# Talking-heads attention with a PReLU block behind it: four shared two-bank PSUM tiles in place of four dedicated ones, full-tile units in the second phase, contiguous group columns, 12 setup loads

## Chip, cores and metric

One core of one Trainium2 chip. The metric is the device time of one execution in microseconds (us). Engines: PE (TensorE: matmuls, its weight loads listed as PEld), DVE (VectorE), ACT (ScalarE), POOL (GpSimd), SP (SyncE, here only a DMA queue).

## What is computed

```python
batch, n_heads, seq, head_dim = (4, 12, 448, 64)
scores = scale * np.matmul(q, k.transpose(0, 1, 3, 2))
scores = np.einsum('bhij,hg->bgij', scores, w_pre)
scores = scores - np.max(scores, axis=-1, keepdims=True)
attn = np.exp(scores)
attn = attn / (np.sum(attn, axis=-1, keepdims=True) + 1e-09)
attn = np.einsum('bhij,hg->bgij', attn, w_post)
x = np.matmul(attn, v)            # then (1792 tokens) x (12 * 64 = 768)
h = x @ w_in                      # 768 x 2048
g = np.maximum(h, 0.0) + alpha * np.minimum(h, 0.0)
out = g @ w_out                   # 2048 x 768
```

The two weights `w_in` and `w_out` come as 64-bit floats, which the kernel rounds to fp32 itself; `q`, `k`, `v`, `w_pre`, `w_post` are fp32.

## The kernel before

The work has two phases that are interleaved by hand: every engine runs its instructions in the order in which the program lists them.

**First phase (attention)**: 90 steps `step(n)`; a step handles one batch of two groups of 10 query rows with all 12 heads. A step has on PE `mix(n)` (L188: the `w_pre` product, from `sr` tiles that DMAs of the SP queue, `relay`, have rearranged), `post(n-1)` (L222: the `w_post` product of the step before, which also divides by the sum), and, when due, `qk` (L160: scores of a chunk of 60 rows, three calls per chunk, placed by the table `qk_at`) and `pv` (L241: the product with `v`, two halves, some steps after a list of chunks is complete). Each is read out of PSUM by another engine: `rmax` (DVE, L193, one per step) and `exp` (ACT, L200) read `mix`; `post_out` (ACT, L231, two copies with strided columns) reads `post`; `qk_out` (L167) and `pv_out` (L249 and L250) read `qk` and `pv`. `norm(n)` (DVE, L206 to L210) makes the factors `r` that `post(n)` multiplies by, and needs the sums of `exp(n)`.

**Second phase (the two-layer block)**: the tokens are cut into four blocks `TB` (300, 498, 498, 496). A block can start when the attention rows it needs are stored to DRAM (`READY`); while the steps run, `moe_work` gives it a share of PE per step, `PACE`, in ns at full clock. Block 0 (`moe0`) multiplies in fp32, the others (`moe`) in three fp32r products with weights split into two parts (`split_w`: ACT cast L306, POOL subtract L307). The first layer (`l1`, L342 or L381) accumulates one of 16 column slices `f` and is read by DVE and ACT (L312, L394 to L396: the PReLU and the split of `g`); the second (`l2`, L360 or L408) accumulates for two slices one of 6 output slices `c` at a time, and DVE adds the result to `acc` (`add_out`, L320). One such piece is called a unit here. While the steps of `n <= ready[0]` run (the lead), no second-phase work is done, and `converts` rounds weights on DVE and POOL (L58 to L65). The last block can only run after the last step.

**PSUM** is eight banks in four tiles of two banks, each with its own use:

```python
PM = ps.tile([128, 2, 512], F32, name="m")     # mix
PS_ = ps.tile([128, 2, 512], F32, name="s")    # qk, first half of pv
PA = ps.tile([128, 2, 512], F32, name="pa")    # post, second half of pv
PW = ps.tile([128, 2, 512], F32, name="h")     # second phase (odd mixes in the lead)
banks = [PW[:, 0], PW[:, 1]]                   # a unit takes one bank, in turn
```

After the last step the other tiles' banks join the list, so that block 3 goes through eight banks in turn.

Of the kernel before, what the change touches and what calls it, by code (L numbers as in the profile page):

```python
# [22 lines left out]
HI = 5  # L23
HP = HI * H
# [12 lines left out]
WARM = (12, 8)  # L37
# [5 lines left out]
PACE = (3800.0, 5000.0, 5200.0)  # L43
CONV_LEAD, CONV_T0 = 4, 8
F0 = 8

# [22 lines left out]
def talking_heads_prelu(ctx: ExitStack, tc: tile.TileContext, q, k, v, w_pre, w_post, mask, w_in, w_out, alpha, out):  # L69
# [8 lines left out]
    groups = [(ci, g) for ci, (b, c) in enumerate(chunks) for g in range(CHUNKS[c][1] // GI)]  # L78
# [5 lines left out]
    for b, lists in enumerate(PVS):  # L84
        for cs in lists:
            r0 = CHUNKS[cs[0]][0]
            cn = sum(CHUNKS[cs[-1]]) - r0
            base = AW - cn if lists[-1] == cs == (len(CHUNKS) - 1,) else 0
            for c in cs:
                a_col[place[b, c]] = base + CHUNKS[c][0] - r0  # L90
            pvs.append((b, r0, cn, base, lb[place[b, cs[-1]]]))
# [92 lines left out]
    def mix(n, to):  # L184
# [40 lines left out]
    def post_out(n):  # L225
        for g in range(2):
            ci, j = groups[2 * n + g]
            nh = CHUNKS[chunks[ci][1]][1] // HI
            cols = a_t.rearrange("p s h i -> p (s h) i")[:, :, a_col[ci]:a_col[ci] + nh * HI]
            dst = cols.rearrange("p s (i u) -> p s u i", u=nh)[:, :, 2 * j:2 * j + 2]  # L230
            nc.scalar.copy(dst, PA[:, g, :NS * GP].rearrange("p (s u i) -> p s u i", u=2, i=HI))  # L231

    def pv(i, hx, to):
        b, r0, cn, base, _ = pvs[i]
        for cl in range(3):
            for s in range(NS):
                for t in range(2):
                    h = 2 * (3 * hx + cl) + t
                    for r in range(2 if 2 * s + 1 < NJ else 1):
                        pr = slice(64 * r, 64 * r + 64)  # L240
                        nc.tensor.matmul(to[64 * t:64 * t + 64, r, cl * AW:cl * AW + cn],  # L241
                                         v_t[b, hx][pr, s, (2 * cl + t) * D:(2 * cl + t + 1) * D],
                                         a_t[pr, s, h, base:base + cn], start=(s == 0), stop=(2 * s + 2 + r >= NJ))

    def pv_out(i, hx, to):
        b, r0, cn, base, _ = pvs[i]
        xe = xep.tile([128, 3, AW], F32, tag="xe", name=f"xe{i}_{hx}")
        src = to[:, :, :3 * AW].rearrange("p r (c i) -> p r c i", c=3)
# [39 lines left out]
    turn = [0]  # L288
# [389 lines left out]
```

## Time and profile before

| | us |
|---|---|
| median of 3 runs | 1534.86 (1532.36 to 1535.69) |
| profiled execution | 1545.28 |
| its span | 1543.5 |
| mean granted TensorE clock | 0.802 of 2.4 GHz |
| busy: PE, DVE, ACT, POOL | 1106.9, 560.2, 472.4, 397.0 |

The profiled execution is 0.7% above the median of the runs, and 1.8 us above its own span. PE is the busiest engine; its busy time is at the clock granted, which has two levels, 1.2 and 2.4 GHz, so that the same matmul can stand there with one duration or with twice that.

### The profile page before, as it was taken

What the parts mean: (1) busy time and instruction counts of PE and PEld (TensorE: products, weight loads), DVE (VectorE), ACT (ScalarE), POOL (GpSimd) and SP (SyncE); (2) the same over time, 40 slices, a digit from 0 to 9 for tenths busy, and PEclk for the clock granted to TensorE, in tenths of its full rate; (3) what the DMA queues carried; (4) which work ended last, traced back from release to release, by engine and by line L of the source; (5) the groups of instructions that cost most, each with busy time, mean ns of one, the idle gap of its engine ahead of it and who ended that gap; (6) DMA issues with size and microseconds to landing.
All of it is one profiled execution on the core that took longest, in us unless ns stands there. A gap on an engine that the chain in (4) does not pass through costs nothing. (4 is left out here: it accounts for less than half of the span.)

```text
span 1543.5 us, 28060 instructions
## 1 busy us (share of the span) xinstructions
PE 1106.9 (72%) x12012; PEld 727.5 (47%) x12012; DVE 560.2 (36%) x969; ACT 472.4 (31%) x837; POOL 397.0 (26%) x433
## 2 busy tenths in 40 slices
PE   3566555786776676877778777787877867687777
PEld 1244323453433434545445545554554645465555
DVE  2767645223434323222223333323232233233333
ACT  1344413232221223443323432343333322131111
POOL 6423433011111101222202322312221212243431
PEclk6668778788866877878768897697876879789999
DMA  6655665232323223422212322422221201322211
GB/s 156 225 177 191 193 220 161 99 111 71 108 90 111 83 95 113 121 69 90 73 35 84 111 69 91 149 75 78 69 75 43 90 28 52 113 68 78 72 51 40
DMA packets 73899, 155.45 MB, mean 101 GB/s; under 512 B 25700, under 2 KB 55408, under 8 KB 73776
## 3 DMA queue, kind: packets, MB, share of 16 engines
q0 software_dynamic: 20032, 84.29, 19.5%
q1 hardware_dynamic: 52812, 67.96, 12.6%
q8 instruction: 94, 1.54, 0.4%
q10 hardware_dynamic: 932, 1.43, 0.3%
q14 instruction: 29, 0.24, 0.0%
HBM read 91.33 MB, written 23.59 MB: 74 GB/s over the span
## 5 line engine op out<-in xcount | busy, mean ns | idle before, releaser
L307 POOL TENSOR_TENSOR ws<-wr,ws 128x768 fp32r<-128x768 f32 x96 | 175.7, 1831 | 657.8 <-ACT ws L306 656.9
L231 ACT COPY at<-pa 128x480 f32<-128x480 f32 x180 | 168.4, 1041 | 524.8 <-PE pa L222 524.8
L408 PE MATMUL h<-g,ws 128*128 128x498 f32 (+1 forms) x666 | 224.0, 482 | 90.7 <-DVE acc L320 52.0
L381 PE MATMUL h<-xs,ws 128*128 128x498 f32 (+1 forms) x612 | 205.9, 493 | 67.0 <-DVE t L394 33.2
L408 PEld LDWEIGHTS h<-g,ws 128*128 128x128 f32 x666 | 144.7, 231 | 167.5 <-DVE acc L320 79.1
L381 PEld LDWEIGHTS h<-xs,ws 128*128 128x128 f32 x612 | 141.9, 243 | 131.8 <-issue 34.9
L160 PE MATMUL s<-k,q 64*64 64x448 f32 x752 | 115.9, 656 | 82.6 <-ACT st L167 67.0
L320 DVE TENSOR_TENSOR acc<-h,acc 128x498 f32<-128x498 f32 (+2 forms) x139 | 85.3, 614 | 245.3 <-PE h L408 174.3
L222 PEld LDWEIGHTS pa<-r,e 64*64 64x64 f32 x5040 | 115.8, 155 | 110.7 <-issue 82.9
L222 PE MATMUL pa<-r,e 64*64 64x60 f32 x5040 | 117.9, 243 | 51.5 <-DVE r L210 42.0
L193 DVE TENSOR_REDUCE nm<-m 128x2 f32<-128x896 f32 x82 | 89.3, 1090 | 172.4 <-PE m L188 172.4
L188 PE MATMUL m<-sr,wk 64*64 64x448 f32 (+1 forms) x656 | 104.9, 698 | 0.0
L200 ACT ACTIVATE e<-m,nm 128x448 f32<-128x448 f32 x164 | 102.2, 636 | 6.8 <-DVE nm L193 6.8
L167 ACT COPY st<-s 128x896 f32<-128x896 f32 x87 | 80.2, 922 | 65.3 <-DMA sr<-st 33.5
L306 ACT CAST ws<-wr 128x768 fp32r<-128x768 f32 x96 | 78.0, 840 | 68.6 <-issue 56.9
L300 POOL DMA_DIRECT2D wr<-wsc x112 | 62.6, 560 | 110.6 <-PE h L360 51.3
L395 ACT CAST g<-t 128x498 fp32r<-128x498 f32 (+1 forms) x48 | 29.2, 609 | 172.5 <-DVE t L394 172.5
L160 PEld LDWEIGHTS s<-k,q 64*64 64x64 f32 x752 | 27.1, 153 | 104.3 <-ACT st L167 83.9
L206 DVE TENSOR_SCALAR s<-se 128x2 f32<-128x2 f32 x90 | 19.3, 215 | 148.7 <-ACT e L200 148.5
L360 PE MATMUL h<-g,w 128*128 128x300 f32 x96 | 45.9, 620 | 31.6 <-DVE acc L320 20.8
L59 POOL TENSOR_SCALAR ce<-ce 128x768 int32<-128x768 int32 x32 | 32.0, 999 | 139.3 <-DVE ce L58 136.9
L381 PE MATMUL m<-xs,ws 128*128 128x496 f32 x252 | 59.6, 389 | 9.8 <-DVE t L394 9.8
(86 smaller groups left out, 1204.0 us busy)
## 6 DMA issues: line engine op xcount, KB each, us to landing
wr<-wsc POOLq DMA_DIRECT2D x112, 384.0 KB, 3.6
sr<-st SPq DMA_DIRECT2D x330, 105.0 KB
cr<-in_w_in_dram POOLq DMA_DIRECT2D x16, 768.0 KB, 5.3
cr<-in_w_out_dram POOLq DMA_DIRECT2D x16, 768.0 KB, 5.3
wsc<-w SPq DMA_DIRECT2D x32, 384.0 KB
q<-in_q_dram POOLq DMA_DIRECT2D x54, 90.0 KB, 3.8
v<-in_v_dram POOLq DMA_DIRECT2D x8, 576.0 KB, 6.3
x<-xe SPq DMA_DIRECT2D x24, 180.0 KB
```

The lines of the kernel that those rows point to most:

```text
L160: nc.tensor.matmul(pt[64 * cc:64 * cc + 64, r, :S], q_t[ci][h, (3 * cc + p) * cn + SR0 * cc:(3 * cc + p) * cn + SR0 * cc + 64], k_t[b, p][ ...
L167: copy(s_t[ci][:, :, p, :], pt[:, :, :S])
L188: nc.tensor.matmul(to[hf:hf + 64, u, :S], wk[r, :], g[r, :], start=True, stop=True)
L193: nc.vector.tensor_reduce(out=nm, in_=m_t[n][:, :, :S], axis=AX.X, op=ALU.max, negate=True)
L200: nc.scalar.activation(out=e_t[n][:, u], in_=m_t[n][:, u, :S], func=AF.Exp, bias=nm_t[n][:, u:u + 1], scale=1.0, accum_out=se_t[n][:, u:u ...
L222: nc.tensor.matmul(dst[:, :, HI * u:HI * u + HI], e[h, u, 64 * jb:64 * jb + 64], r[h, u].rearrange("p (h i) -> p h i", h=H), start=True, s ...
L231: nc.scalar.copy(dst, PA[:, g, :NS * GP].rearrange("p (s u i) -> p s u i", u=2, i=HI))
L306: nc.scalar.copy(t[:, 0], w)
L307: nc.gpsimd.tensor_tensor(t[:, 1], w, t[:, 0], ALU.subtract)
L320: nc.vector.tensor_tensor(acc_o[:, c, :N], pt[:, :N], acc_o[:, c, :N], ALU.add)
L381: nc.tensor.matmul(pt[:, :N], w[:, tw, c * 128:(c + 1) * 128], xs[:, tx, c, :], start=(j == 0), stop=(j == 3 * NCC - 1))
L408: nc.tensor.matmul(pt[:, :N], w[:, tw, c * 128:(c + 1) * 128], g[:, tg], start=(j == 0), stop=(j == 3 * FG - 1))
```

## The change

Four two-bank tiles `p0` to `p3` replace the dedicated ones. `grab()` gives the one that was freed longest ago in program order, `free()` gives it back right after its readers are listed. A unit of the second phase fills a whole tile: `l1` takes two slices `f`, `l2` two output slices `c`, with one DVE instruction over both banks to add them; `order()` puts `l2` of a pair one pair of `l1` later. The columns of a group lie next to each other in `at`, so that `post` is read out by one ACT copy for both groups where they belong to one chunk (88 of the 90 steps; the un-permuting moves to the read-out of `pv`). In a step `exp(n)` now always follows `post(n-1)`, `norm(n)` stands behind two thirds of the step's second-phase work, and `qk` is not placed in steps with `pv`. The setup loads go from 28 to 12, two memsets go to POOL, the first `qk` stands ahead of `wk`, and fewer of the first relays go through ACT's queue. Pace, conversion rate and ready steps change too.

```diff
-PACE = (3800.0, 5000.0, 5200.0)
-CONV_LEAD, CONV_T0 = 4, 8
+PACE = (4200.0, 5600.0, 5600.0)
+CONV_LEAD, CONV_T0 = 4, 4
...
+    pairs = [ps.tile([128, 2, 512], F32, name=f"p{i}") for i in range(4)]
+    age = [0, 1, 2, 3]
+    clock = [4]
+    def grab():
+        i = min((i for i in range(4) if age[i] is not None), key=lambda i: age[i])
+        age[i] = None
+        return pairs[i]
+    def free(t):
+        age[next(i for i in range(4) if pairs[i] is t)] = clock[0]
+        clock[0] += 1
...
+    def mix(n):
+        to = m_t[n] = grab()
...
+        nc.vector.tensor_reduce(out=nm, in_=to[:, :, :S], axis=AX.X, op=ALU.max, negate=True)
...
+        free(m_t.pop(n))            # in exp(n)
...
+        if ca == cb:                # in post(n)
+            col = a_col[ca] + GI * ja
+            nc.scalar.copy(at[:, :, col:col + 2 * GI].rearrange("p q (g i) -> p g q i", g=2),
+                           pt[:, :, :NS * GP].rearrange("p g (q i) -> p g q i", i=GI))
...
     def add_out(t, G, c, pt, N):
+        dst = acc_o[:, c:c + 2, :N]
         if G == 0:
-            nc.scalar.copy(acc_o[:, c, :N], pt[:, :N])
+            nc.vector.tensor_copy(dst, pt[:, :, :N])
         else:
-            nc.vector.tensor_tensor(acc_o[:, c, :N], pt[:, :N], acc_o[:, c, :N], ALU.add)
+            nc.vector.tensor_tensor(dst, pt[:, :, :N], dst, ALU.add)
+        free(pt)
...
+        seq = [("l1", 0), ("l1", 1)]
+        for G in range(NG2 - 2):
+            seq += [("l2", G), ("l1", G + 2)]
+        return seq + [("l2", NG2 - 2), ("l2", NG2 - 1)]
...
+                pt = grab()         # moe, l1
+                for f in fs:
...
+                            nc.tensor.matmul(pt[:, f % 2, :N], w[:, tw, c * 128:(c + 1) * 128], xs[:, tx, c, :],
...
+                        for f1 in fs:
+                            prelu(P, t, f1, pt, N)
+                        free(pt)
...
+                for c in range(0, NCC, 2):          # moe, l2
+                    pt = grab()
+                    for d in range(2):
...
+                                nc.tensor.matmul(pt[:, d, :N], w[:, tw, (c + d) * 128:(c + d + 1) * 128], g[:, tg],
...
-    ready = [pvs[i][4] + 2 for i in READY]
+    ready = [pvs[i][4] + 3 for i in READY]
...
-                for i in range(HI):
-                    nc.gpsimd.dma_start(out=wb[o + NP * i:o + NP * i + NP, 0, :], in_=pre[c])
+                nc.gpsimd.dma_start(out=wb[o:o + HP // 2, 0, :], in_=wide(w_pre[NP * c:NP * c + NP], NP))
...
+            if live(n):             # in step(n)
+                mix(n)
             if due is not None:
...
             if live(n - 1):
                 post(n - 1)
...
+            if live(n):
                 exp(n)
...
+            else:
+                moe_work(n, pace * 0.4)
+                if cur == 0:
+                    converts(min(CONV_T0 // 2, room()))
+                moe_work(n, pace * 0.25)
             if live(n):
                 norm(n)
...
-                moe_work(n, pace)
+                moe_work(n, pace * 0.35)
```

How this moves instructions, at three places. First PE, in the second layer of block 1. Names: `m`, `pa`, `s`, `h` are the dedicated tiles, `p_119` to `p_122` the shared ones. Before:

```order
L188 MATMUL m<-sr_113,wk 64x448 x2
L222 MATMUL pa<-r_4697,e_4636 64x12x5 x28
L160 MATMUL s<-k_2_3843,q_114 64x448 x4
L408 MATMUL h<-g_0_4413,ws_1_4488 128x498 x3
L408 MATMUL h<-g_1_4509,ws_1_4499 128x498 x3
...
L381 MATMUL h<-xs_4367,ws_0_4516 128x498 x6
L188 MATMUL m<-sr_106,wk 64x448 x2
```

Now:

```order
L172 MATMUL p_122<-k_2_3779,q_114 64x448 x4
L410 MATMUL p_121<-xs_4345,ws_0_4551 128x498 x18
L442 MATMUL p_119<-g_0_4558,ws_1_4574 128x498 x3
L442 MATMUL p_119<-g_1_4564,ws_1_4590 128x498 x3
...
L200 MATMUL p_120<-sr_106,wk 64x448 x2
L200 MATMUL p_120<-sr_107,wk 64x448 x2
L233 MATMUL p_122<-r_4696,e_4647 64x12x5 x28
L172 MATMUL p_121<-k_0_3530,q_115 64x448 x4
```

Before, every row of the second phase writes `h`, three units of six matmuls there in a row. Now neighbouring pieces on PE write different tiles, and a unit of the second layer has twelve matmuls.

Second DVE, in a step of block 1 with second-layer units. Before:

```order
L206 TENSOR_SCALAR s_5336<-se_5273 128x2
L207 RECIPROCAL s_5336<-s_5336 128x2
L210 TENSOR_TENSOR r_5339<-wq,s_5336 128x120
L320 TENSOR_TENSOR acc<-h,acc 128x498 x2
L193 TENSOR_REDUCE nm_5365<-m 128x2
```

Now:

```order
L202 TENSOR_REDUCE nm_5281<-p_122 128x2
L342 TENSOR_TENSOR acc<-p_119,acc 128x2x498
L342 TENSOR_TENSOR acc<-p_121,acc 128x2x498
L216 TENSOR_SCALAR s_5349<-se_5313 128x2
L217 RECIPROCAL s_5349<-s_5349 128x2
L220 TENSOR_TENSOR r_5352<-wq,s_5349 128x120
L202 TENSOR_REDUCE nm_5362<-p_122 128x2
```

The adds now stand ahead of the three instructions of `norm`, which wait for ACT's sums, instead of behind them.

Third POOL, the setup. Before (these rows come twice):

```order
L462 DMA mask_sb<-in_mask_dram 30x1x60
L464 DMA wb<-in_w_pre_dram 6x1x12 x5
L462 DMA mask_sb<-in_mask_dram 30x1x60
L464 DMA wb<-in_w_pre_dram 6x1x12 x5
L466 DMA mask_sb<-in_mask_dram 60x60
L467 DMA wb<-in_w_post_dram 60x1x12
```

Now (the two `30`-row loads come four times, the other two twice):

```order
L502 MEMSET mask_sb 128x120
L503 MEMSET wb 128x24
L509 DMA mask_sb<-in_mask_dram 30x1x60
L510 DMA wb<-in_w_pre_dram 30x1x12
...
L513 DMA mask_sb<-in_mask_dram 60x60
L514 DMA wb<-in_w_post_dram 60x1x12
```

Five loads of 6 rows have become one of 30.

## Rows read from the trace of the kernel before

**Rows 1.** Busy time of each engine by stretch, whole core, cut at row maxima (L193); last columns: granted clock, DMA share, GB/s.
```profile
0.00:48.30 48.30, 18.73 (x84) 7.05 (x84) 17.43 (x35) 4.91 (x5) 29.82 (x52) 0.68 0.59 159
48.30:188.20 139.90, 79.78 (x1664) 52.40 (x1664) 95.05 (x149) 61.73 (x118) 48.50 (x62) 0.75 0.62 196
188.20:592.80 404.60, 279.01 (x3344) 165.90 (x3344) 152.17 (x275) 110.16 (x207) 70.76 (x95) 0.78 0.37 116
592.80:969.60 376.80, 289.73 (x3188) 190.39 (x3192) 116.76 (x208) 136.23 (x238) 94.25 (x94) 0.82 0.28 85
969.60:1308.80 339.20, 262.28 (x2851) 179.55 (x2845) 102.16 (x186) 114.81 (x203) 75.21 (x68) 0.79 0.24 74
1308.80:1355.00 46.20, 31.70 (x349) 21.93 (x339) 14.64 (x27) 8.84 (x15) 9.50 (x8) 0.76 0.35 105
1355.00:1543.50 188.50, 145.71 (x563) 110.26 (x562) 62.04 (x92) 35.67 (x52) 68.94 (x55) 0.93 0.21 61
```

**Rows 2.** The same view for L193 alone: length, DVE busy (xcount = steps), clock, DMA.
```profile
48.30:188.20 139.90, 18.41 (x17) 0.75 0.62 196
188.20:592.80 404.60, 29.43 (x27) 0.78 0.37 116
592.80:969.60 376.80, 26.17 (x24) 0.82 0.28 85
969.60:1308.80 339.20, 22.89 (x21) 0.79 0.24 74
```

**Rows 3.** PE's groups by line, 593 to 970 us: xcount | busy, mean ns | idle before, releasers.
```profile
L408 PE MATMUL h<-g,ws 128*128 128x498 f32 x288 | 100.5, 496 | 44.6 <-DVE acc L320 23.8 <-DVE t L394 15.6 <-ACT acc L318 3.6
L381 PE MATMUL h<-xs,ws 128*128 128x498 f32 x288 | 89.6, 462 | 24.6 <-DVE t L394 9.6 <-ACT ws L306 4.9 <-DVE acc L320 4.6
```

**Rows 4.** Timeline of one step in block 2: start us, us, engine line op, [idle before <-releaser].
```profile
1250.21 1.88 ACT L231 COPY at<-pa 128x480 f32<-128x480 f32 x2 [2.97 <-PE pa L222]
...
1253.25 0.17 DVE L206 TENSOR_SCALAR s<-se 128x2 f32<-128x2 f32 x1 [2.76 <-ACT e L200]
...
1253.86 0.67 DVE L320 TENSOR_TENSOR acc<-h,acc 128x498 f32<-128x498 f32 x1
...
1254.58 2.86 PE L408 MATMUL h<-g,ws 128*128 128x498 f32 x6 [2.86 <-DVE acc L320]
...
1258.21 2.86 PE L408 MATMUL h<-g,ws 128*128 128x498 f32 x6 [0.77 <-DVE acc L320]
```

**Rows 5.** Timeline in block 3, after the last step, where units go through eight banks.
```profile
1418.19 1.63 PE L408 MATMUL s<-g,ws 128*128 128x496 f32 x6 [2.13 <-DVE acc L320]
...
1419.66 1.50 PE L408 MATMUL pa<-g,ws 128*128 128x496 f32 x6
...
1419.86 0.68 DVE L320 TENSOR_TENSOR acc<-s,acc 128x496 f32<-128x496 f32 x1 [1.72 <-PE s L408]
```

**Rows 6.** One round of block 3 (two slices f), whole core, columns as in the first group.
```profile
1404.57:1427.10 22.53, 17.23 (x73) 13.22 (x72) 8.13 (x12) 4.25 (x7) 9.56 (x8) 1.00 0.25 71
```

**Rows 7.** Timeline of the start.
```profile
12.71 2.78 POOL L464 DMA_DIRECT2D wb<-in_w_pre_dram  x5
...
20.24 0.22 DVE L473 SCALAR_TENSOR_TENSOR wk<-mask_sb,wb 128x60 f32<-128x60 f32 x1 [13.48 <-DMA wb<-in_w_pre_dram]
...
35.80 0.91 ACT L167 COPY st<-s 128x896 f32<-128x896 f32 x1 [24.11 <-DMA sr<-st]
```

**Rows 8.** PE's groups by line, 48 to 188 us (the lead).
```profile
L222 PE MATMUL pa<-r,e 64*64 64x60 f32 x896 | 24.7, 268 | 44.4 <-DVE r L210 36.4 <-ACT st L167 4.9 <-DVE xe L250 3.0
```

**Rows 9.** ACT's groups by line and shape, whole span: two copies out of PSUM.
```profile
L231 ACT COPY at<-pa 128x480 f32<-128x480 f32 x180 | 168.4, 1041 | 524.8 <-PE pa L222 524.8
...
L167 ACT COPY st<-s 128x896 f32<-128x896 f32 x87 | 80.2, 922 | 65.3 <-DMA sr<-st 33.5 <-PE s L160 31.8
```

**Rows 10.** Timeline in block 3: the first and the last DVE step of one slice's PReLU.
```profile
1408.83 0.73 DVE L312 TENSOR_SCALAR t<-m,alpha_sb 128x496 f32<-128x496 f32 x1 [3.38 <-PE m L381]
...
1410.94 0.68 DVE L396 TENSOR_TENSOR g<-t,g 128x496 fp32r<-128x496 f32 x1 [0.67 <-ACT g L395]
```

More of the change, by code (lines that the diff above doesn't have):

```diff
@@ L77, in talking_heads_prelu @@
     place = {bc: ci for ci, bc in enumerate(chunks)}
-    groups = [(ci, g) for ci, (b, c) in enumerate(chunks) for g in range(CHUNKS[c][1] // GI)]
+    half = lambda ci: CHUNKS[chunks[ci][1]][1] // HI
+    groups = [(ci, g) for ci in range(len(chunks)) for g in range(half(ci) // 2)]
     NG, NC = len(groups), len(chunks)
@@ L287, in talking_heads_prelu @@
     wr_t, wi_t, wo_t, g_t, xs_t, xr_t = {}, {}, {}, {}, {}, {}
-    turn = [0]
-    banks = [PW[:, 0], PW[:, 1]]
-    def bank():
-        turn[0] += 1
-        return banks[turn[0] % len(banks)]
+    used, nxt_x = [0, 0], {}
     def load_w(u, x):
@@ L303, in split_w @@
     def split_w(P, u, x):
+        if (u, x) not in wr_t:
+            return
         t = P[x].tile([128, 2, DM], F32R, tag="w", name=f"ws{u}_{x}")
@@ L308, in split_w, with prelu @@
         (wi_t, wo_t)[x][u] = t
[L310 removed]
+    def prelu(P, t, f, pt, N):
         h = tp.tile([128, 512], F32, tag="t", name=f"t{t}_{f}")
[L312 to L313 removed]
+        ps_f = pt[:, f % 2, :N]
+        nc.vector.tensor_scalar(out=h[:, :N], in0=ps_f, scalar1=0.0, scalar2=alpha_sb[:, f:f + 1], op0=ALU.min, op1=ALU.mult)
+        if t == 0:
+            g = P["g"].tile([128, N], F32, tag="g", name=f"g0_{f}")
+            nc.vector.scalar_tensor_tensor(out=g, in0=ps_f, scalar=0.0, in1=h[:, :N], op0=ALU.max, op1=ALU.add)
+        else:
+            g = P["g"].tile([128, 2, N], F32R, tag="g", name=f"g{t}_{f}")
+            nc.vector.scalar_tensor_tensor(out=h[:, :N], in0=ps_f, scalar=0.0, in1=h[:, :N], op0=ALU.max, op1=ALU.add)
+            nc.scalar.copy(g[:, 0], h[:, :N])
+            nc.vector.tensor_tensor(g[:, 1], h[:, :N], g[:, 0], ALU.subtract)
+        g_t[t, f] = g
@@ L421, in split_x @@
         a, N = TB[t]
+        while step_now[0] <= ready[t]:
+            yield
         xs = xs_t[t] = P["xs"].tile([128, 2, NCC, N], F32R, tag="xs", name=f"xs{t}")
@@ L452, in talking_heads_prelu @@
         nc.vector.memset(warm.bitcast(F32), 0.0)
-        for _ in range(WARM[0]):
-            nc.tensor.matmul(PM[:, 0, :], warm[:, :128], warm, start=True, stop=True)
-        nc.vector.memset(mask_sb, 0.0)
-        nc.vector.memset(wb, 0.0)
-        pre = w_pre.rearrange("(r c p) g -> c r p g", r=2, c=2)
+        for _ in range(WARM):
+            nc.tensor.matmul(pairs[3][:, 0, :], warm[:, :128], warm, start=True, stop=True)
+        nc.gpsimd.memset(mask_sb, 0.0)
+        nc.gpsimd.memset(wb, 0.0)
         own = mask[:HP, :HI, :].rearrange("(i h) j g -> i h j g", h=H)
+        wide = lambda w, n: w.rearrange("(o h) g -> o h g", o=1).to_broadcast([HI, n, H])
         for u in range(2):
@@ L482, in talking_heads_prelu @@
         )
-        for p in range(3):
-            pt = qk(0, p, (PS_, PA, PM)[p])
-            qk_out(0, p, pt, nc.vector.tensor_copy if p % 2 else nc.scalar.copy)
-        load_q(2)
+        load_q(1)
         nc.gpsimd.dma_start(out=alpha_sb, in_=alpha)
@@ L492, in relays @@
             nonlocal relayed
-            while relayed < min(upto, NG):
+            while relayed < min(upto, NG) and (groups[relayed][0], NP // 2 - 1) in done_qk:
                 relay(relayed, dmas)
                 relayed += 1
-        relays(2 * (RA + 1) if lb[0] >= RA else 2 * lb[0] + 2, (nc.sync, nc.scalar))
+        relays(4, (nc.sync, nc.scalar))
+        relays(2 * (RA + 1), (nc.sync,))
         next(conv)
-        for hx in range(2):
-            load_v(0, hx)
+        for ci in (2, 3):
+            load_q(ci)
         conv_done, conv_steps, lead_steps = 0, NFC * 2 * 5, F0 * 2 * 5
@@ L558, in step @@
         def step(n):
-            for ci, p in qk_at.get(n, []):
-                if p == 0 and ci + 2 < NC:
-                    load_q(ci + 2)
+            step_now[0] = n
+            if n == 1:
+                for hx in range(2):
+                    load_v(0, hx)
             if n >= 0:
```

304 lines of the change are left out of this document (145 added, 159 removed).

## The prediction

> **What bounds the kernel now.** I read the busy time by stretch first, cut where the stages change [rows 1]: the start to the first row maximum, the lead (17 steps), the steps with block 0 (27), block 1 (24) and block 2 (21), a short change-over, and block 3 alone; the same view for L193 counts the steps [rows 2]. The reader is to see that PE is the busiest engine from 188 us on, but only for 69 to 77% of each stretch, and mostly at a mean granted clock of 0.78 to 0.82. Busy time times clock is what PE would need at 2.4 GHz without a pause: block 0 279.0 x 0.78 = 218 us of 404.6, block 1 289.7 x 0.82 = 238 of 376.8, block 2 262.3 x 0.79 = 207 of 339.2, block 3 145.7 x 0.93 = 136 of 188.5. No other engine is over 40% there. So the loss is pauses and a slow clock on PE, and what makes them is the question.
>
> The groups by line say who ends the pauses [rows 3]: in the block 1 stretch PE idles 44.6 us before L408 and 24.6 before L381, of 87 in all (376.8 - 289.7), mostly for DVE's reads, `acc` and `t`. The timeline shows it happening. Every second-layer unit on `h` waits 0.77 us for DVE's add of the unit before [rows 4], although the two lie in different banks: the wait is for the tile. Block 3 proves that: the second unit on `s` waits for the add, the next one, on `pa`, starts at 1419.66 while the add of `s` only starts at 1419.86 [rows 5]. Once per step it is worse: the add stands on DVE behind `norm`, `norm` waits for ACT's `exp`, `exp` stands behind the two copies of `post`, and PE pauses 2.86 us [rows 4]. After that pause six matmuls take 2.86 us, where they take 1.63 in block 3: PE is back at 1.2 GHz, and with 0.77 us lost after each unit it is still there two units later.
>
> The lead is another matter: DVE is busy 95.1 of 139.9 us there, PE 79.8, and PE's largest wait is for `r` of `norm` [rows 1, 8]. And the start is a chain of small loads: `wk` waits 13.48 us for `wb`, whose loads POOL issues at about 0.56 us each, and ACT's next copy waits 24.11 us behind relays [rows 7].
>
> **The change part by part.** All against the profiled execution (1545.3 us, span 1543.5; the median of the runs is 0.7% lower).
>
> *Setup.* 16 loads fewer on POOL at 2.78 / 5 = 0.56 us are 9 us [rows 7]; the first score copies no longer stand behind `wk`, and two of six groups leave ACT's relay queue. I take the start from 48.3 to 26 us; bounds 22 (all of the 24.11 us wait, and 2 more) and 40 (the 9 us alone).
>
> *The lead* is one step longer (ready + 3 for + 2), so 18 steps to the first with block 0. A step is 139.9 / 17 = 8.2 us now. Conversions stay on DVE; the two 1.04 us copies of `post` become one of 960 elements. The contiguous runs have no row; the bounds are 960 / 896 x 0.92 = 0.99 us, as the contiguous copy of scores goes, and 2 x 1.04 = 2.08 [rows 9]. I take 1.3, nearer to the first, since what differs from it (runs of ten) is small; 0.8 us less between `post` and `exp`, of which I credit 0.6: 18 x 7.6 = 137 us (117 to 148).
>
> *Blocks 0 to 2.* A tile is taken again only after three others, so PE has another piece between a unit and its tile's reuse: the 0.77 us waits go, and so do the equal ones between two first-layer slices. The read of a pair costs at most two adds of 0.68 us, 1.36 [rows 5], less than the 12 matmuls of the next pair. The adds now stand ahead of `norm`, and `norm` has a third of the step's second-phase work behind it, so the 2.86 us pause should go too. What is late next: the PReLU of a pair is twice a chain of DVE, ACT and DVE, 2.8 us for one slice [rows 10], and `rmax` and the `post` copy queue behind it. When the tile ring comes round to that tile first, PE waits some 1.4 us, and `post` may wait another 1 us for a late `norm`. That happens in about one step of three; with smaller waits elsewhere I put 1 us of pause on each step (bounds 0.3, and half of the present idle). With pauses that short the clock should stay at 2.4 GHz most of the time: block 3 at present has 5.3 us of pauses in a round of 22.53, none longer than 2.2, at a clock of 1.00 [rows 5, 6]. I take 0.95. Then block 0 is 218 / 0.95 + 27 = 256 us, block 1 238 / 0.95 + 24 = 274, block 2 207 / 0.95 + 20 = 238 (27, 24 and 20 steps; the higher pace only moves work within a block, since each still waits for its rows and idles 2 to 4 steps before). DVE's conversions in block 0 are halved per step and spread; they stay hidden as long as DVE, 152 us busy of 404.6, has room in 256 [rows 1]. The first adds of a block go from ACT to DVE, 12 pairs of at most 1.36 us, hidden in the same room. Un-permuting `pv` reads (40 halves, on ACT and DVE) at worst goes as the strided copy, 1.04 / 480 per element: 0.78 us for 360 elements, hidden by the other half's matmuls.
>
> The Trainium skill bears on this (Perfetto Trace Analysis, section Matmuls): independent groups should rotate through different PSUM banks so that the read-out overlaps. Its sentence would call the kernel before already right, since neighbouring units change banks; the rows differ, and a rotation by banks overlapped nothing within a tile. By the page there would be nothing to win in the blocks, and that is one of the rivals.
>
> *Change-over and block 3.* 46.2 us become 40, fewer waits before the same DMA round trip. A round of block 3 is 17.2 us of PE at full clock against some 24 per round on average (188.5 / 8 = 23.6) [rows 1, 6]. With four tiles in rotation nothing should wait: 8 x 17.5 + 4 for the last add and store = 144 us (140 to 165).
>
> Sum: 26 + 137 + 256 + 274 + 238 + 40 + 144 = 1115 us of span, 1117 with the 1.8 around it, and 0.7% less for a median: **1110 us**.
>
> **The rivals.**
>
> *The waits go, the clock doesn't follow.* PE keeps today's busy time in the blocks and 1 us of pause per step: 279 + 27, 290 + 24, 262 + 20; with 26, 137, 42 and 150: 1257 us, 1250 as a median. For it: the lead and the blocks have low clocks also where attention's small matmuls run. Against: block 3's 0.93 with 23% idle. The Trainium skill has a rule on that side (TensorE: Matmul & The Clock Gate, "A second HAM failure mode: psum-queue depth-cycling"): cycling through PSUM banks in each iteration leaves pauses between groups, and the clock oscillates. Block 3's rows, eight banks in turn at 1.00 for a round, do not agree.
>
> *New waits take the place of old ones*: one ring couples all uses, and half of the present idle stays at today's clock: 342 + 333 + 301, with 30, 145, 46 and 165: 1362, 1355 as a median.
>
> *The wait is not the tile's*: if a unit waits for the add before it whatever tile it writes, pairs halve the number of waits (0.77) but make each longer by the second half of the add (0.68): next to nothing is won in the blocks, and start and lead bring about 25 us: some 1510. The start of `pa` in [rows 5] speaks against it. This is also what the page's sentence would give.
>
> *Slower: the clock falls in every step.* PE's order is fixed, so one pause a step on a ring tile whose reader is queued behind a PReLU pair on DVE and ACT could, like the 2.86 us one, drop PE to 1.2 GHz each time, and the work of a step no longer recovers. At 0.50 the blocks take 435 + 27, 475 + 24, 414 + 20, with 26, 137, 46 and 160: 1764, 1750 as a median. It decides from a clock of 0.60 in the three blocks: (218 + 238 + 207) / 0.60 + 71 + 369 = 1545. For it: the chain of a pair is 5.6 us, longer than any now. Against: its tile has three others ahead of it in the ring.
>
> **How the numbers follow.** Forecast 0.70, clock not following 0.16, new waits 0.06, not the tile 0.03, slower 0.05. The forecast's own low end: pauses of 0.3 us, clock 1, 22 + 117 + 226 + 245 + 213 + 34 + 140 = 997, so the range begins at 1000; its upper side reaches into the second case, and 1300 leaves out what is above, about 0.14, and a little below. Faster by over 0.2% (what a measurement of this kernel can tell from no change): 0.94; within: 0.01; slower: 0.05.
>
> **What would show it.** Right: PE's idle before second-layer matmuls nearly gone, no 0.77 us wait between neighbouring units, rounds of block 3 near 17.5 us, a granted clock above 0.9 in the blocks, steps of 10 to 12 us instead of 15 to 16, `at` copies of 1.0 to 1.5 us, the first row maximum at about 26 us. Wrong: idle moved to `mix`, `post` or first-layer rows with ACT or DVE as releasers; a clock of 0.8 in spite of few pauses; a lead step that stays at 8 us or more because DVE binds it; block 0 held by conversions.

## The result, and the profile after

The changed kernel takes 1104.18 us (median of 4 runs, 1099.07 to 1104.7) against 1535.03 for the kernel before beside it: a ratio of 0.7188, 95% interval 0.7165 to 0.7211. Its profiled execution has a span of 1102.4 us and a mean granted clock of 0.907, for 0.802 before.

Busy time by stretch of the changed kernel, cut at the same places as [rows 1] except for the last (columns as there; the start to the first row maximum, the lead of 18 steps, blocks 0, 1 and 2 with 27, 24 and 20 steps, the change-over, block 3), and below it one round of block 3, as [rows 6]:

```profile
0.00:25.50 25.50, 15.88 (x61) 7.19 (x65) 10.32 (x28) 4.00 (x4) 15.69 (x30) 0.75 0.73 179
25.50:165.10 139.60, 87.38 (x1764) 56.52 (x1756) 99.49 (x158) 53.03 (x109) 49.94 (x66) 0.75 0.69 214
165.10:405.70 240.60, 213.55 (x3352) 143.53 (x3352) 147.59 (x261) 88.70 (x178) 68.79 (x96) 0.94 0.62 192
405.70:687.10 281.40, 240.87 (x3283) 173.94 (x3284) 121.13 (x191) 115.58 (x209) 101.48 (x101) 0.93 0.42 125
687.10:924.40 237.30, 209.22 (x2708) 154.92 (x2704) 110.61 (x173) 92.62 (x171) 76.93 (x68) 0.94 0.34 102
924.40:953.30 28.90, 17.18 (x300) 13.26 (x292) 6.32 (x12) 5.27 (x10) 4.73 (x4) 0.79 0.32 105
953.30:1102.40 149.10, 138.67 (x576) 111.13 (x576) 69.29 (x83) 33.77 (x46) 69.22 (x55) 0.95 0.28 84
...
1011.24:1027.48 16.24, 16.24 (x74) 13.53 (x73) 7.93 (x9) 4.46 (x6) 9.62 (x9) 1.00 0.34 98
```

Here block 3 begins with its first matmul. [rows 1] cut it at 1355, 9.2 us after the first matmul of block 3 in the kernel before, so only the sum of change-over and block 3 can be compared, 234.7 and 178.0 us:

```profile
1345.79 3.05 PE L381 MATMUL h<-xs,ws 128*128 128x496 f32 x6 [4.52 <-DVE xs L425]
```

The three blocks give 361 of the 441 us of span: 1120.6 became 759.3. They idle less on PE (290 us became 96) and the same matmuls are shorter, because the clock rose. The round of block 3 shown has no pause left. The lead, though one step longer, takes what it took.

PE's groups by line in the stretch of block 1, where [rows 3] had 44.6 and 24.6 us of idle time for the two layers:

```profile
L442 PE MATMUL p<-g,ws 128*128 128x498 f32 x288 | 76.2, 421 | 10.2 <-DVE t L331 3.4 <-ACT ws L318 3.1 <-POOL ws L319 2.2
L410 PE MATMUL p<-xs,ws 128*128 128x498 f32 x288 | 73.2, 406 | 8.7 <-ACT at L239 6.9 <-DVE xs L463 1.5 <-DVE xs L464 0.3
L233 PE MATMUL p<-r,e 64*64 64x60 f32 x1344 | 29.7, 229 | 19.1 <-DVE r L220 17.6 <-issue 1.4
```

Of the 48 second-layer units of the stretch one waits for an add, 1.5 us; before, 24 units did, 23.8 us in all (half of them, not every one as the prediction has it). The largest idle of the stretch has moved to `post` (L233), which waits for `r` nine times. The timeline of the changed kernel (start us, us, engine line op, [idle before <-releaser]) shows two waits: a second-layer unit around 514 us, and `post` around 864 us:

```profile
513.94 2.41 DVE L333 TENSOR_TENSOR g<-t,g 128x498 fp32r<-128x498 f32 x1 [0.67 <-ACT g L332]
513.99 1.81 POOL L319 TENSOR_TENSOR ws<-wr,ws 128x768 fp32r<-128x768 f32 x1
...
517.03 0.68 DVE L331 SCALAR_TENSOR_TENSOR t<-p,t 128x498 f32<-128x498 f32 x1
...
517.76 7.23 PE L442 MATMUL p<-g,ws 128*128 128x498 f32 x24 [3.40 <-DVE t L331]
...
518.38 0.68 DVE L333 TENSOR_TENSOR g<-t,g 128x498 fp32r<-128x498 f32 x1 [0.67 <-ACT g L332]
...
856.77 0.21 ACT L209 ACTIVATION_READ_ACCUMULATOR e<-p,nm 128x1 f32 x1
...
857.67 0.74 DVE L325 TENSOR_SCALAR t<-p,alpha_sb 128x498 f32<-128x498 f32 x1 [2.81 <-PE p L410]
...
863.64 1.19 DVE L342 TENSOR_TENSOR acc<-p,acc 128x996 f32<-128x996 f32 x1
...
864.75 0.16 DVE L216 TENSOR_SCALAR s<-se 128x2 f32<-128x2 f32 x1
...
865.14 0.28 DVE L220 TENSOR_TENSOR r<-wq,s 128x120 f32<-128x120 f32 x1
...
865.48 1.09 PE L233 MATMUL p<-r,e 64*64 64x60 f32 x54 [1.48 <-DVE r L220]
```

The sums of `exp` are there at 857 us, but `norm` (L216 to L220) is written behind the PReLU of two slices, from 857.67 on, and an add. DVE reaches it at 864.75, PE has meanwhile run out of other work, and `post` waits 1.48 us. At 517.76 the second layer itself waits 3.40 us for a pair of slices: L331 of the second slice ends at 517.71, and the only thing that it and L442 share is the PSUM tile, which comes round in the ring after `mix`, `post` and `qk`. This wait occurs once in block 1 and once in block 2.

### The profile page after: what moved, and what is told of

Its sections match the earlier page's. It is cut to its first block, busy times and chain, and to the rows that moved or that the text cites. A ratio compares the mean times of both kernels' runs of the same rounds, so it can differ in the third digit from the quotient of the medians.

```text
span 1102.4 us, 27933 instructions
## 1 busy us (share of the span) xinstructions
PE 922.7 (84%) x12012; PEld 660.5 (60%) x12012; DVE 564.7 (51%) x898; ACT 393.0 (36%) x725; POOL 386.8 (35%) x419
## 4 chain that ended last, share of the span: by engine, by line
PE 61%; DVE 17%; DMA 8%; issue 5%; ACT 4%; POOL 4%; SPq 0%; POOLq 0%; DVEq 0%; ACTq 0%
PE p L410 16%; PE p L442 14%; PE p L233 8%; PE p L172 7%; PE p L256 6%; PE p L365 4%; PE p L200 3%; PE p L384 3%; DVE g L333 3%; DMA xr<-x 3%; DVE acc L342 2%; DMA cr<-in_w_in_dram 2%; DVE t L325 2%; DVE t L331 2%; ACT g L332 2%
## 5 line engine op out<-in xcount | busy, mean ns | idle before, releaser
L442 PE MATMUL p<-g,ws 128*128 128x498 f32 (+1 forms) x864 | 221.8, 413 | 24.6 <-POOL ws L319 8.4
L410 PE MATMUL p<-xs,ws 128*128 128x498 f32 (+1 forms) x864 | 220.4, 409 | 23.9 <-DVE xs L463 16.4
L442 PEld LDWEIGHTS p<-g,ws 128*128 128x128 f32 x864 | 172.5, 202 | 76.4 <-POOL ws L319 12.1
L410 PEld LDWEIGHTS p<-xs,ws 128*128 128x128 f32 x864 | 166.4, 197 | 77.3 <-DVE xs L463 21.3
L233 PE MATMUL p<-r,e 64*64 64x60 f32 x5040 | 117.8, 238 | 95.2 <-DVE r L220 84.3
L233 PEld LDWEIGHTS p<-r,e 64*64 64x64 f32 x5040 | 109.5, 148 | 143.9 <-issue 94.8
L202 DVE TENSOR_REDUCE nm<-p 128x2 f32<-128x896 f32 x90 | 97.6, 1085 | 69.3 <-PE p L200 69.2
L172 PE MATMUL p<-k,q 64*64 64x448 f32 x768 | 115.9, 652 | 7.4 <-DVE acc L342 2.1
L209 ACT ACTIVATE e<-p,nm 128x448 f32<-128x448 f32 x180 | 112.6, 634 | 20.4 <-DVE nm L202 20.3
L200 PE MATMUL p<-sr,wk 64*64 64x448 f32 x720 | 101.7, 590 | 9.9 <-DMA sr<-st 4.7
L176 ACT COPY st<-p 128x896 f32<-128x896 f32 x88 | 78.2, 915 | 25.5 <-DMA sr<-st 20.6
L333 DVE TENSOR_TENSOR g<-t,g 128x498 fp32r<-128x498 f32 (+1 forms) x48 | 49.5, 1031 | 33.4 <-ACT g L332 33.4
```

What stands on the lines that cost most here:

```text
L172: nc.tensor.matmul(pt[64 * cc:64 * cc + 64, r, :S], q_t[ci][h, (3 * cc + p) * cn + SR0 * cc:(3 * cc + p) * cn + SR0 * cc + 64], k_t[b, p][ ...
L200: nc.tensor.matmul(to[hf:hf + 64, u, :S], wk[r, :], g[r, :], start=True, stop=True)
L202: nc.vector.tensor_reduce(out=nm, in_=to[:, :, :S], axis=AX.X, op=ALU.max, negate=True)
L333: nc.vector.tensor_tensor(g[:, 1], h[:, :N], g[:, 0], ALU.subtract)
L410: nc.tensor.matmul(pt[:, f % 2, :N], w[:, tw, c * 128:(c + 1) * 128], xs[:, tx, c, :], start=(j == 0), stop=(j == 3 * NCC - 1))
L442: nc.tensor.matmul(pt[:, d, :N], w[:, tw, (c + d) * 128:(c + d + 1) * 128], g[:, tg], start=(j == 0), stop=(j == 3 * FG - 1))
```

## The experiments

Stages in us, from the span of one profiled execution each, cut as above ("rest" is everything from the last step on). Every kernel was measured beside the kernel before, so the ratio is what compares two kernels:

| kernel | median | ratio to before, 95% | start | lead | block 0 | block 1 | block 2 | rest |
|---|---|---|---|---|---|---|---|---|
| before | 1535 | 1 | 48.3 | 139.9 | 404.6 | 376.8 | 339.2 | 234.7 |
| changed | 1104.2 | 0.7188 [0.7165, 0.7211] | 25.5 | 139.6 | 240.6 | 281.4 | 237.3 | 178.0 |
| e9 two tiles for `h` | 1216.9 | 0.7917 [0.7881, 0.7953] | 48.7 | 140.4 | 295.6 | 278.5 | 232.1 | 210.7 |
| e1 ring only | 1076.8 | 0.7016 [0.6967, 0.7065] | 48.8 | 127.3 | 264.3 | 246.2 | 215.2 | 171.7 |
| e2 dedicated pairs | 1317.8 | 0.8585 [0.8513, 0.8657] | 25.7 | 154.4 | 304.2 | 357.6 | 292.2 | 181.4 |
| e3 one-bank units | 1075.2 | 0.7002 [0.6950, 0.7053] | 25.9 | 141.4 | 252.8 | 259.1 | 218.4 | 175.4 |
| e4 `norm` first | 1084.0 | 0.7058 [0.7004, 0.7112] | 25.5 | 142.5 | 245.2 | 268.9 | 224.4 | 178.5 |
| e6 = e3 and e4 | 1063.5 | 0.6928 [0.6897, 0.6959] | 26.1 | 141.7 | 259.1 | 255.3 | 208.2 | 173.6 |
| e5 28 loads | 1105.1 | 0.7204 [0.7176, 0.7232] | 30.3 | 138.4 | 238.5 | 279.4 | 237.9 | 177.5 |
| e7 ring, new start | 1070.1 | 0.6965 [0.6941, 0.6989] | 38.9 | 126.8 | 266.3 | 245.8 | 215.0 | 171.7 |
| e8 = e6, lead of 17 | 1065.0 | 0.6945 [0.6914, 0.6975] | 25.1 | 132.7 | 257.5 | 258.0 | 225.0 | 161.4 |
| e10 = e6, strided columns | 1083.0 | 0.7040 [0.7006, 0.7073] | 25.6 | 146.3 | 268.9 | 258.6 | 209.4 | 175.2 |
| e11 = e6, half the conversions | 1051.6 | 0.6860 [0.6834, 0.6886] | 26.1 | 109.7 | 274.2 | 255.1 | 208.1 | 173.9 |
| e12 = e11, paired adds | 1044.4 | 0.6798 [0.6767, 0.6829] | 26.5 | 107.7 | 266.5 | 252.2 | 208.2 | 176.0 |

**Is it the tile?** e9 leaves the kernel before as it is, except that `h` is two tiles:

```diff
-    PW = ps.tile([128, 2, 512], F32, name="h")
+    PH = [ps.tile([128, 512], F32, name=f"h{i}") for i in range(2)]
...
-    banks = [PW[:, 0], PW[:, 1]]
+    banks = [PH[0], PH[1]]
...
-                mix(n, PW if lead and n % 2 else PM)
+                mix(n, PM)
```

> The kernel before with one edit: the two banks of `h` are two tiles of one bank each, still used in turn by the second phase and by nothing else (the odd steps of the lead, which mixed into `h`, mix into `m`). No ring. Theory (the wait is the tile's): a unit then waits only for the read of the last but one, which is over when its neighbour's matmuls end; the 0.77 us waits vanish in blocks 0 to 2, the 2.86 us one in each step stays in part, so the time falls by more than half of what the ring brings: 1250 to 1380 us. Rival (the gain is the number of buffers, not the tile: two are too few for DVE's delays): over 1420. Rival (the wait is not the tile's): 1520 to 1560, the 0.77 us waits stay.

It came out better than the theory's range. The same two banks are used in the same turn; the only thing that changed for a unit is which reads it waits for. PE's second-layer group in block 1, and a stretch of its timeline in block 2:

```profile
L408 PE MATMUL h<-g,ws 128*128 128x498 f32 x288 | 82.3, 436 | 11.8 <-DVE t L394 4.2 <-DVE acc L320 3.5 <-POOL ws L307 3.2
```
```profile
842.10 3.00 PE L408 MATMUL h<-g,ws 128*128 128x498 f32 x12
845.10 1.25 DVE L320 TENSOR_TENSOR acc<-h,acc 128x498 f32<-128x498 f32 x2
845.82 1.64 PE L408 MATMUL h<-g,ws 128*128 128x498 f32 x6 [0.72 <-DVE acc L320]
```

Two units run on without a pause (x12), where [rows 4] have a wait after each six; the wait for adds fell from 23.8 us to 3.5, and the granted clock in the blocks rose to 0.88 to 0.96. The 0.72 us of the third unit is what is left of the pause once per step (2.86 us in [rows 4]): both adds stand on DVE behind `norm`, but PE has had two units to work on. So the 0.77 us waits are the tile's, and the clock rises when they go. These three lines alone bring 318 of the 431 us.

**The ring.** e1 (first diff) gives the kernel before the ring of four tiles, `grab` and `free` around every use, and nothing else; a unit takes one bank of a tile. e2 (second diff) is the changed kernel without the ring while the steps run: each use has its own tile again, with units in pairs. The diffs show the main lines.

```diff
-        pt = to if to is not None else PS_
+        pt = grab()
...
-        return banks[turn[0] % len(banks)]
+        t = grab()
+        return t, t[:, turn[0] % 2]
```
```diff
-    def grab():
-        i = min((i for i in range(4) if age[i] is not None), key=lambda i: age[i])
+    def grab(use=3):
+        if steps_done[0]:
+            i = min((i for i in range(4) if age[i] is not None), key=lambda i: age[i])
+        else:
+            i = use
...
-        to = m_t[n] = grab()
+        to = m_t[n] = grab(0)
```

> The kernel before with one part of the change alone: four tiles that all uses take in turn; a unit of the second phase still fills one bank, and the order of every engine's work, the strided copies and the setup stay. My theory (the wait is for the whole tile, and the slow clock follows from the pauses): most of the gain comes from this, 1150 to 1320 us, granted clock in the three blocks 0.88 or more, no 0.77 us wait between neighbouring units. Rival (the size of a unit, or the place of norm, is what counts): above 1400 us, clock still near 0.8.

> The changed kernel with the ring alone undone: while the steps run, mix, qk and first pv half, post and second pv half, and the second phase have a tile each, as before; units still fill a whole tile, order and setup as changed. My theory: each second-phase unit waits for the read of the one before (1.2 us for an add of a pair, over 4 us for two slices of the PReLU), the clock in the blocks falls to 0.80 to 0.86, 1250 to 1450 us. Rival (pairs and the new order are enough): below 1180 us.

The ring alone is faster than the whole change, which none of the expectations held; e2 is in its theory's range. PE's groups of e1 in block 1:

```profile
L398 PE MATMUL p<-xs,ws 128*128 128x498 f32 x288 | 76.5, 414 | 6.6 <-DVE xs L444 6.5 <-DVE xs L445 0.2
L426 PE MATMUL p<-g,ws 128*128 128x498 f32 x288 | 72.3, 401 | 4.3 <-POOL ws L322 3.2 <-ACT at L244 0.9 <-ACT ws L321 0.2
L234 PE MATMUL p<-r,e 64*64 64x60 f32 x1368 | 27.2, 220 | 0.9 <-DVE acc L335 0.7 <-DVE r L221 0.2
```

`post` waits 0.9 us where the changed kernel has 19.1, and L426 idles 4.3 for 10.2. What the ring adds to e9 in this block is mostly at `qk`, whose calls of a step share one tile in e9. First e9, then e1:

```profile
L160 PE MATMUL s<-k,q 64*64 64x448 f32 x216 | 28.6, 574 | 17.5 <-ACT st L167 17.5
```
```profile
L168 PE MATMUL p<-k,q 64*64 64x448 f32 x216 | 26.5, 549 | 2.3 <-ACT at L244 2.3
```
With dedicated tiles for pairs (e2) the waits are back, now for the PReLU of a pair:

```profile
L448 PE MATMUL p<-g,ws 128*128 128x498 f32 x288 | 94.2, 489 | 48.1 <-DVE t L337 33.8 <-DVE acc L348 9.0 <-POOL ws L325 2.2
L178 PE MATMUL p<-k,q 64*64 64x448 f32 x224 | 32.2, 623 | 27.3 <-ACT st L182 27.3
```

So something else in the change loses part of what the ring gives.

**What the change gives back.** e3 is the changed kernel with one slice or one output unit per tile; e4 has `norm` ahead of the step's second-phase work; e6 has both. One hunk of e3, then the whole of e4:

```diff
-                for c in range(0, NCC, 2):
+                for c in range(NCC):
                     pt = grab()
...
+            if live(n):
+                norm(n)
             if not lead:
                 moe_work(n, pace * 0.4)
...
-            if live(n):
-                norm(n)
```

> The changed kernel with units of one bank on the ring (one slice f or c per tile). My theory: the ring has slack for this too, within 2% of the changed kernel, 1085 to 1130 us, DVE some 15 us busier. Rival (full tiles are what hides the read): above 1180 us.

> The changed kernel with norm back ahead of all second-phase work of its step. My theory: DVE's adds then wait for exp again, but with the ring PE has other tiles; 10 to 50 us more, 1115 to 1155 us. Rival (the place of norm was the larger part of the gain): above 1250 us, pauses near 2.9 us before second-phase units.

> The changed kernel with both edits of the two runs before that were faster: one-bank units on the ring, and `norm` ahead of the step's second-phase work. Theory (both take DVE work from ahead of `norm`: a pair's four PReLU operations and two adds are one long piece, and `norm` stands behind them; `post` waits for `r`): the two gains overlap in part, 1055 to 1068 us, `post` idles under 4 us for `r` in block 1. Rival (each of the two alone already takes the whole wait away): no more than either alone, 1072 to 1085. Rival (they interfere: one-bank adds then stand behind `norm`): over 1085.

Each alone is faster than the change, by 2.6% and 1.8% (0.7002 and 0.7058 over 0.7188), e3 by more than its expectation and e4 against its own in sign. Together they save 41 us, as the theory of e6 had it; alone they save 29 and 20, and whether they overlap is not clear of the intervals. `post` in block 1 waits 9.2 us for `r` in e3 and 2.3 in e4, for 17.6; in e4 L442 still waits for `t`:

```profile
L442 PE MATMUL p<-g,ws 128*128 128x498 f32 x288 | 75.0, 416 | 13.3 <-DVE t L331 3.4 <-ACT ws L318 3.1 <-DVE acc L340 2.7
L233 PE MATMUL p<-r,e 64*64 64x60 f32 x1344 | 27.5, 221 | 3.8 <-DVE r L220 2.3 <-issue 1.3 <-ACT st L176 0.2
```

Which of the two pairs costs, e12 tells: on e11 (below) it puts back the paired output units with their one add (996 elements in blocks 1 and 2), and leaves slices one to a tile.

> The kernel of the last job with half of the conversions ahead of block 0 (1051.6 us: one-bank units, `norm` first), with the second-layer units of the changed kernel put back: pairs of 12 matmuls that fill a tile and one add of 992 elements for two; the first-layer slices stay one to a tile. It tells which of the two pairs costs. Theory (it is the pair of slices: their two PReLU chains stand on DVE in one piece, and their tile is held for 72 matmuls, across a step's attention): the pair of adds costs nothing, 1043 to 1056 us. Rival (it is the adds: one read of 1.09 us instead of two of 0.68 us, each of which frees a tile sooner): 1060 to 1080, with blocks 1 and 2 longer by 10 or more together.

```profile
L438 PE MATMUL p<-g,ws 128*128 128x498 f32 x288 | 71.7, 402 | 6.0 <-ACT ws L318 3.1 <-POOL ws L319 2.5 <-DVE acc L340 0.4
L233 PE MATMUL p<-r,e 64*64 64x60 f32 x1344 | 27.2, 220 | 3.5 <-DVE r L220 2.3 <-issue 1.1
```

Paired adds are no cost, with `norm` first as in both e11 and e12; e12 is 7 us below e11, mostly in block 0. That leaves the pair of slices as what loses in blocks 1 and 2, by exclusion: its PReLU is one piece on DVE and ACT, and its tile is held until both slices are done. In block 0 it is the other way round: one-bank units cost 12 us there (e3 against the changed kernel) and 14 (e6 against e4), and the paired adds of e12 give only 8 of that back. A kernel with pairs of slices in block 0 alone was not run. e12 is the best kernel of the study, 5.4% under the changed one (0.6798 / 0.7188).

**Start and lead.** e5 issues the 16 setup loads again; e7 gives e1 the new start (12 loads, score copies ahead of `wk`, and the lines of the second diff); e8 lets each block begin one step earlier than e6; e11 is e6 with half the conversions ahead of block 0.

```diff
-                nc.gpsimd.dma_start(out=wb[o:o + HP // 2, 0, :], in_=wide(w_pre[NP * c:NP * c + NP], NP))
+                for i in range(HI):
+                    nc.gpsimd.dma_start(out=wb[o + NP * i:o + NP * i + NP, 0, :], in_=w_pre[NP * c:NP * c + NP])
...
```
```diff
+        nc.gpsimd.memset(mask_sb, 0.0)
+        nc.gpsimd.memset(wb, 0.0)
...
+        relays(4, (nc.sync, nc.scalar))
+        relays(2 * lb[0] + 2, (nc.sync,))
```
```diff
-    ready = [pvs[i][4] + 3 for i in READY]
+    ready = [pvs[i][4] + 2 for i in READY]
```
```diff
-F0 = 8
-CONV_LEAD, CONV_T0 = 4, 4
+F0 = 4
+CONV_LEAD, CONV_T0 = 2, 6
```

> The changed kernel with five six-row loads of the pre weight in each half instead of one broadcast load: 28 setup loads on POOL, 16 more. Theory (the loads are a chain on POOL, 0.56 us of issue each, and `wk` waits for the last): the first row maximum moves from 25.5 to about 34 us, the rest stays, 1104 becomes about 1112 us. Rival (the copies' wait behind `wk` and the relays made the long start, not the loads): first row maximum stays within 2 us of 25.5, time within 3 us of 1104.

> The ring alone (1077 us) with the changed kernel's start: 12 setup loads, the first score copies ahead of `wk`, two of the relays' groups on SP alone. Theory (the start's gain is independent of the ring and adds to it): first row maximum from 48.8 to 26 to 28 us, the rest as in the ring alone, 1052 to 1058 us. Rival (what the start wins is lost again in the lead, which waits for the same loads of q, k and x on the DMA queues): lead longer than 127 us by 10 or more, 1065 to 1078.

> The one-bank, norm-first kernel of this job with the second phase begun one step earlier, as in the kernel before (row 2 of the ready rule for 3): 17 lead steps instead of 18. Theory (a lead step is 7.8 us, most of it not filled; the work that it holds goes on beside block 0): 5 to 8 us less than the kernel with 18. Rival (block 0 then waits for its rows, or the conversions that the step held come on top in block 0): within 3 us of it.

> The one-bank, norm-first kernel with half of the conversions ahead of block 0: 4 of 24 slices converted in the start and the lead instead of 8, two pieces a step instead of four, and six instead of four a step beside block 0. Theory (the lead's step of 7.8 us is bound by DVE, which is busy 99.5 of its 139.6 us, mostly with conversions): the lead falls from 140 to about 115 us, block 0 grows by 10 to 20 as DVE has less room there, 1045 to 1062 us. Rival (the lead step is the chain of a group, relay to `mix` to `exp` to `norm` to `post`, not DVE): lead within 5 us of before, block 0 longer, 1070 or more.

(The slices are 16, not 24.) The 16 loads move the first row maximum by 4.8 us, not 9, the end of the lead by 3.6, and the time by nothing that can be told (0.7204 and 0.7188). e7's time is in the rival's range, but not for the rival's reason: the lead is as long as in e1, and the first row maximum comes at 38.9, not 26. The timeline of e7 shows why. PE has finished the first `mix` at 28.8, and the row maximum stands on DVE behind conversions and the weights that they wait for:

```profile
26.28 2.56 PE L199 MATMUL p<-sr,wk 64*64 64x448 f32 x8 [1.82 <-DVE st L176]
...
32.80 0.56 DVE L58 TENSOR_SCALAR ce<-cr 128x768 int32<-128x768 int32 x1 [5.72 <-DMA cr<-in_w_out_dram]
33.28 0.55 DVE L62 TENSOR_SCALAR w<-cr 128x768 int32<-128x768 int32 x1
33.87 1.46 DVE L63 SCALAR_TENSOR_TENSOR w<-cr,w 128x768 f32<-128x768 uint32 x1
...
37.04 0.96 DVE L65 TENSOR_TENSOR w<-w,ce 128x768 f32<-128x768 f32 x1
...
38.85 1.09 DVE L204 TENSOR_REDUCE nm<-p 128x2 f32<-128x896 f32 x1
```

The old loop begins three steps ahead of the first, each with four pieces of conversion, and they stand ahead of the row maximum on DVE; the changed loop begins one step ahead and has one step more of lead. So of the 22.8 us that the start became shorter, some 13 (38.9 - 25.5) go with the later conversions: part is their work on DVE, which is now done in the lead, and part the 5.72 us that DVE waits for their weights. What is won by the end of the lead is 10.4 us (176.1 in e1, 165.7 in e7); the medians differ by 6.6 us, which the two intervals do not tell from nothing. e8 is 11.5 us ahead of e6 at the end of block 0 (415.3 for 426.9) and level with it in the end, as its rival had it: block 2, with 21 steps for 20, is 16.8 us longer and the rest 12.2 shorter; why was not followed. Fewer conversions do shorten the lead: the stretches of lead and block 0, first of e6, then of e11.

```profile
26.11:167.81 141.70, 87.40 (x1765) 56.84 (x1757) 99.61 (x157) 53.09 (x109) 50.05 (x66) 0.74 0.69 210
167.81:426.86 259.05, 215.39 (x3352) 145.79 (x3352) 149.77 (x285) 88.82 (x177) 71.21 (x97) 0.93 0.56 178
```
```profile
26.12:135.80 109.68, 77.40 (x1762) 47.30 (x1755) 67.64 (x122) 51.98 (x108) 28.32 (x41) 0.86 0.65 197
135.80:409.97 274.17, 220.70 (x3352) 147.34 (x3352) 184.63 (x324) 89.75 (x178) 90.46 (x111) 0.92 0.59 186
```

DVE has 32 us less in the lead and the lead is 32 us shorter; PE's waits for `r` there fall from 46.8 to 16.0 us. So the conversions on DVE bind the lead. (POOL's part of them fell too, by 22 us, and was not separated.) Block 0 takes 35 us more of DVE work and gets 15 us longer.

**Contiguous columns.** e10 is e6 with two strided copies to `at` again.

```diff
+        for g in range(2):
...
+            dst = cols.rearrange("p s (i u) -> p s u i", u=nh)[:, :, 2 * j:2 * j + 2]
+            nc.scalar.copy(dst, pt[:, g, :NS * GP].rearrange("p (s u i) -> p s u i", u=2, i=HI))
```

> The one-bank, norm-first kernel (1063.5 us) with the columns of a group strided again: two copies of 480 elements to `at` in each step, as before the change, in place of one of 960, and `pv` reads in order. Theory (the copies are 2 x 1.04 us on ACT against 0.98, 1.1 us a step, ahead of `exp` in the chain of a step, and the lead is bound by DVE, ACT has room in the blocks): 0 to 8 us slower. Rival (the copy is on the path of every step): 90 x 1.1 = 99 us at most, 20 or more slower. Rival (nothing: other work covers it all): within 3 us.

It is 17 to 19 us slower (0.0112 of 1535, or 1083.0 - 1063.5), between the theory and the rival that has the copy on every step's path. Some 14 of that lie in the lead (4.6) and block 0 (9.8). ACT's groups of lead and block 0, first e6, then e10:

```profile
L239 ACT COPY at<-p 128x960 f32<-128x960 f32 x43 | 42.1, 978 | 162.9 <-PE p L233 145.5 <-DVE acc L342 12.4 <-DVE w L66 3.7
```
```profile
L240 ACT COPY at<-p 128x480 f32<-128x480 f32 x88 | 81.8, 1034 | 157.8 <-PE p L233 140.8 <-DVE acc L338 13.3 <-DVE w L66 3.7
```

A step's copying is 1.09 us shorter when contiguous (2 x 1.034 - 0.978), 49 us over these 45 steps; the kernel gets some 14 us longer there, with the order of the `pv` reads, which changed along with the copies.

## Why the prediction came out

The forecast was 1110, the time is 1104, and the mechanism held: waits that belong to a tile, not to a bank, and a clock that recovers when they are gone (e9, e1, the 16.24 us round at 1.00). All four rivals fall by their numbers. Of the second, new waits in the place of old ones, a part is true: a third of the old idle time is left (96 of 290 us), not half, and the largest of it stands at `post`, which the prediction had among its signs of being wrong. The Trainium skill's sentence on rotating banks (Perfetto Trace Analysis, Matmuls) is not enough here: before and e9 rotate the same two banks, at 1535 and 1217 us. The Trainium skill's warning of cycling through PSUM banks (TensorE: Matmul & The Clock Gate, "A second HAM failure mode: psum-queue depth-cycling") is not borne out by any run: every ring kernel has 0.91 to 0.97 in the blocks.

The terms, predicted and measured: start 26, 25.5; lead 137, 139.6; block 0 256, 240.6; block 1 274, 281.4; block 2 238, 237.3; change-over and block 3 together 184, 178.0 (28.9 and 149.1; by the cut of [rows 1], about 38 and 140, for 40 and 144). That the sum fits within 1% is in part luck: block 0 came out 15 us under its term and block 1 seven over. Behind it several steps were wrong:

- **"so the 2.86 us pause should go too", by the place of `norm`.** The pause went, but because of the tiles: with `norm` where it was, no second-layer unit of block 1 waits more than 0.7 us for an add in e9, and none waits for one in e1. The new place costs: 17.6 us of waits for `r` in block 1, and e4 is 20 us faster. I had put "another 1 us for a late `norm`" into one step of three; the share was right (nine of 24 steps), but the wait is 2.0 us on average, 0.6 to 3.3.
- **Pairs.** That the read of a pair hides under the next 12 matmuls is right for the adds (e12). For slices I named the risk, some 1.4 us when the ring comes round to their tile. That wait is 3.40 us, of which 1.73 (2.41 - 0.68) come with POOL's work (last section), but there is only one in block 1. The larger cost is `norm` behind two chains of PReLU. All pauses together, 1 us a step in the forecast, are 27.1, 40.5 and 28.1 us in the blocks, 1.0, 1.7 and 1.4 a step.
- **"Busy time times clock is what PE would need."** It overstates. The same measure after is 201, 224 and 197 us (213.55 x 0.94 and so on) for the 218, 238 and 207 that I summed with. The stretches do not hold quite the same work (block 2 has a step less and more second-phase matmuls), but the whole kernel, 12012 matmuls in both, shows it too: 1106.9 x 0.802 = 888 before, 922.7 x 0.907 = 837 after. Why was not followed. That error of 41 us hid the idle time that I had too low, and the clock of 0.93 to 0.94 for 0.95.
- **Start.** The sum was right, the parts were not: the 16 loads are 4.8 us, not 9, and more than half of the shorter start comes from conversions that no longer stand ahead of the first row maximum, which the prediction did not name.
- **Lead.** The `at` copy took 0.98 us, not 1.3, and the step is still 7.76 us for 7.6: the copy was credited with 0.6 us a step, and e10 shows 4.6 us in 18 steps, about 0.3, because DVE binds the lead (e11). The text had that as a sign of being wrong, at 8 us or more.
- **Block 3.** Rounds are shorter than forecast (16.24 for 17.5), but its first 72 matmuls took 23.4 us (953.30 to 976.72) for the 16.24 of 72 in a later round: PE has waited 6.51 us for the split of `x` before them, and the first six take 3.15 us, where six take 1.4 in a later round (16.24 / 12).

Left open: whether block 1 would fall from e12's 252 to e1's 246 us with the old order of a step around it. That was not tried, nor were the later place of `l2` (`order()`), the new pace and the new table of `qk` by themselves. In e10 the strided copies and the order of the `pv` reads were not separated.

## What to carry to other kernels

Look at which object a wait is kept for: two buffers in one tile were one buffer here, and splitting that tile brought 318 of the 431 us, before any new schedule. After that, put short work that PE waits for (here `norm`) ahead of long in-order work on the same engine, and, where that work is long, hand the tile back after each slice (blocks 1 and 2; in block 0 pairs were better). A stage that gets shorter may only have passed its work on: follow the end of the next stage before crediting it.

## What the runs showed of the hardware

DVE's subtraction that splits `g` (L333, two operands in SBUF) has no fixed price. In the changed kernel it takes 0.68 us when POOL computes nothing, and up to 2.41 us beside POOL's subtraction of the weight split, as at 513.94 above, where POOL's instruction takes 1.81. Of its 48 executions the 24 fastest, all of 0.68 us, overlap with no computation on POOL; the other 24, of 0.71 to 2.41 us, all do. L331, which reads one operand from PSUM, takes 0.67 to 0.68 us with or without POOL beside it. I had priced the chain of a pair from a row without POOL work [rows 10]; at 513.94 it is one cause of the 3.40 us that PE waits. The Trainium skill agrees (SBUF — State Buffer, "SBUF: two separate sides"): a DVE instruction with two SBUF inputs and a GpSimd one that reads SBUF exclude each other for a whole instruction.
